# One PSUM tile of eight banks in place of two fixed pools, casts on GpSimd in halves, and a new order of work

## The chip, the cores and the metric

The kernel runs on one core of a Trainium2 chip. The time is that of one execution on the device, in microseconds (us). Five engines work side by side, each through a queue of its own in strict order: TensorE for matmuls (PE in the profile; PEld is its weight load), VectorE (DVE), ScalarE (ACT), GpSimd (POOL) and SyncE (SP), which here only issues DMAs. PE writes to PSUM, which has eight banks of 128 partitions x 512 fp32. DVE and ACT read it; POOL's operations here work on SBUF alone.

## The reference

Two steps follow each other. The first is attention over 4 batches of 8 heads, 768 positions and 64 dimensions, in which a position sees the 96 positions up to itself and the first 8 positions of its sequence, with a bias that falls with distance. The second is a feed-forward layer over all 3072 tokens, with three input matrices, of whose products the elementwise maximum is taken.

```python
scores = scale * np.matmul(q, k.transpose(0, 1, 3, 2)) - slopes * dist      # per head
scores = np.where(is_global | is_local, scores, -1e9)
a = softmax(scores)                                                          # over keys
x = np.matmul(a, v)                                  # to (3072, 512)
h = np.maximum(np.maximum(x @ w1, x @ w2), x @ w3)   # 512 -> 768
out = h @ w_out                                      # 768 -> 512
```

Inputs and output are fp32; the matmuls take bf16.

## The kernel before

Tokens are cut into 24 tiles T of 128 (six for each batch), and two neighbouring tiles make a pair G. The feed-forward layer takes the tiles in seven chunks of 4, 2, 2, 4, 4, 4 and 4 tiles, so that attention for a chunk must be done before its first feed-forward matmul.

The order is written out: SCHEDULE is a list of some 760 units that a planner has put in order, and the last lines of the function call one short function for each. A unit is a letter, its arguments and, behind "@", the buffer that it takes. On each engine the instructions run in the order of the list; semaphores between engines are put in by the tile framework. So a unit waits for its inputs, for its buffer to be released, and for everything ahead of it in its engine's queue. Where the last argument chooses the engine, 0 is ACT, 1 is DVE and 2 is POOL.

The units, by the line of their main instruction:

- l (lines 190 and 197): load of q, k or v (first argument 0 for q, 1 for k, 2 for v) for a pair, 512 KB. "12" as the pair stands for the first 512 positions of batch 0, which are loaded in four pieces (q and k, each in two halves of heads).
- c (205, 210): cast of a load to bf16. v (215): the same for half a tile of v.
- x (229, 235): eight PE transposes of a cast half into a PSUM bank. y (243, 246): copy of that to SBUF as qkT. From pair 5 on X (251) is used instead, a transposing DMA.
- S (301): scores of a tile for half of the heads (g), eight 64-row matmuls into two banks; four for the first tile of a batch. Where its last argument is 1, two matmuls with a bias come first (293), and no m follows.
- e (308): exp of the scores on ACT, into P. m (317, 319): P times a mask on DVE. K (330) and B (325) make masks and biases at the start.
- G (266, 268) and V (279, 281): the eight global rows of k and v, kept or put in the place of rows that the next tile doesn't need. So G of a tile waits for its S, and V of a tile for its A.
- A (343, 346): P times v, sixteen matmuls of 65 columns into two banks. n (354, 355): the result divided by the row sums, into xb.
- t (370) and u (373): four PE transposes of xb and a copy to xT; Z (376) is a transposing DMA that does the same.
- F (385): one sixth f of the width of one of the three products j of a chunk, four matmuls 512 wide (256 wide in the two short chunks) into one bank. f: for j = 0 a copy to SBUF (399), for j = 1 (401) and j = 2 (404) the maximum with it, always on DVE.
- O (409): output of a tile, six matmuls. o (424): its copy, s its store. E (406 to 415): the outputs of the last chunk.
- w, W (466, 470) and q, Q (475, 478): load and cast of the feed-forward weights. D, d (484): dummy matmuls on zeros, where PE would wait. R: the start of the mask's distances.

So "F0.4.0@3" is chunk 0, sixth 4, product 0, into bank 3 of its pool.

Two pools share PSUM. Pool "h" has four slots of one bank, for F, O, x, t and D; pool "sp" has two slots of two banks, for S, A and d:

```python
pools[name] = ctx.enter_context(tc.tile_pool(name=f"p_{name}", bufs=1, **space))
...
return pools[name].tile(shape, dtype, name=label, tag=f"{name}{slot}")
```

The first F of chunk 0 needs attention of tiles 0 to 3 and the first weights; until then the order holds the casts, transposes, S, A and so on of four tiles. Behind it F and O fill PE, with S, A, x and t of the coming chunks put between them.

Of the kernel before, what the change touches and what calls it, by code (L numbers as in the profile page):

```python
# [24 lines left out]
    l1.12.0@0 l0.12.0@1 R K3 K7 K4 B1.0 K2 K6 K1 K0 K5 B5.1 B3.1 B0.0 c1.12.0.1@0 B2.1 l1.12.1@2 l0.12.1@3  # L25
    c0.12.0.1@1 B7.1 l2.0.2@0 v1.0.2 v0.1.2 l2.1.2@1 v0.0.2 l1.2.2@4 D10.512@0 D1.256@1 x12.1.0@1 y0.1.0.0@0
    v1.1.2 y1.1.0.1@1 D3.256@2 x12.0.0@2 l0.2.2@5 y0.0.0.0 S0.0.1@0 c1.12.1.1 e0.0@0 S1.0.0@1 w0.0@0
    c0.12.1.1 v3.1.2 w0.1@1 x12.1.1@3 D5.256@0 x12.0.1@0 v2.1.2 e1.0@1 y0.1.1.0 w0.2@2 y0.0.1.0 d4.256@0
    S0.1.0@0 G0.0 e0.1@2 v3.0.2 S1.1.0@1 v2.0.2 c1.2.2.2@2 e1.1@3 w1.0@0 y1.1.1.1 y1.0.0.1 y1.0.1.1 w1.1@1
    l2.2.2@2 G1.1 D3.256@1 S2.0.1@0 e2.0@4 m0.1.1 D2.256@1 A0@1 m1.0.1 n0@0 D3.256@1 S2.1.0@0 m1.1.1 G2.0  # L30
    e2.1@5 D2.256@1 S3.1.0@1 t0@1 m2.1.1 e3.1@6 u0.1@0 D4.256@3 A1@0 n1@1 S3.0.1@1 c0.2.2.1 l0.3.2@6 V1.0
    D2.256@3 A2@0 V2.2 x2.1.2@3 e3.0@7 w1.2@2 m3.1.1 x2.0.2@2 y2.1.2.0@2 A3@1 n2@2 W0.1.2 V3.2 t2@0 n3@3
    u2.1 y2.0.2.0 W0.0.2 t1@1 D4.256@3 t3@3 W2.0.2 G3.0 u1.0 l1.3.2@0 u3.1 B4.0 S4.0.0@0 S4.1.0@1 e4.1@0
    G4.0 W1.1.2 v4.1.2 q2@1 m4.1.1 e4.0@2 W0.2.0 F0.0.1@2 F0.1.1@0 F0.1.0@1 F0.0.0@3 f0.1.0.1@0 l2.3.2@0
    m4.0.1 f0.0.0.0@1 S5.1.0@1 v4.0.2 S5.0.0@0 F0.0.2@1 f0.1.1.1 F0.1.2@3 F0.4.0@0 e5.0@1 f0.0.1.1
    f0.0.2.1@0 f0.1.2.1 W1.0.0 e5.1@3 m5.0.1 W2.1.1 l1.4.2@1 F0.5.0@2 f0.5.0.1@2 c0.3.2.2@0 v5.0.0 v5.1.0
# [49 lines left out]
"""  # L86

SIZES = [4, 2, 2, 4, 4, 4, 4]
RINGS = {'r': 7, 'rv': 3, 'qb': 3, 'qkT': 4, 'sp': 2, 'h': 4, 'P': 8, 'xb': 4, 'xT': 3, 'wst0': 3, 'wst1': 3, 'ht': 2, 'h01': 5, 'rz': 4}

LAST_BANKS = (1, 3, 0, 2)


@with_exitstack
def kernel(
# [43 lines left out]
    def ring(name, slot, shape, dtype, label):  # L139
        assert 0 <= slot < RINGS[name]  # L140
        return pools[name].tile(shape, dtype, name=label, tag=f"{name}{slot}")
# [422 lines left out]
```

## Time and profile before

| | |
|---|---|
| runs of the kernel before | 177.62, 178.47 and 178.69 us, median 178.47 |
| the profiled execution | 178.06 us, of which its span 176.3 |
| granted TensorE clock in it | 0.999 |
| busy: PE, DVE, ACT, POOL | 166.8, 131.2, 107.6, 46.1 us |
| first feed-forward matmul (L385) | starts at 23.52 us |
| last copy on ACT (L414) | starts at 173.04 us |
| HBM read and written | 25.17 MB and 6.29 MB, 178 GB/s over the span |

The span is one execution as the profiler saw it; the time of the execution is 1.8 us more. In the rows of the profile, times are us from the start of the span unless ns is said. A timeline row gives start, length, engine, line, operation and operands, how many instructions are merged in it, and in brackets how long the engine had been idle and what ended that. A row of busy time by stage gives the stretch and its length, then busy time and instructions of PE, PEld, DVE, ACT and POOL, then the granted clock, the DMA engines' busy share and GB/s. The chain of waits goes back from the last instruction, at each step to what released it; "issue" in it is time in which nothing that the profile shows was waited for. A matmul's length includes the time for which it still runs while the next has been started, so PE's queue is read by steps from start to start.

### The profile page before, as it was taken

To read this page: it belongs to the slowest core of one execution; us is meant where nothing else is said; L and a number is where in the kernel's file an instruction comes from. 1 tells how busy PE (TensorE), PEld (TensorE's weight loads), DVE (VectorE), ACT (ScalarE), POOL (GpSimd) and SP (SyncE) were. 2 spreads that over 40 slices of the span, in tenths; PEclk is the share of its full clock that TensorE was granted. 3 is DMA by queue.
4 is the path that set the end of the run, shared out by engine and by line. 5 is a ranking of instruction groups with operands and counts; after the bars stand their busy time and mean duration, and the time that the engine had idled before them with its cause. 6 is when DMAs were issued, how large, how long until landed. Compare 5 with 4: busy or idle time off the path is not lost.

```text
span 176.3 us, 3882 instructions
## 1 busy us (share of the span) xinstructions
PE 166.8 (95%) x1504; PEld 94.3 (53%) x1525; DVE 131.2 (74%) x258; ACT 107.6 (61%) x166; POOL 46.1 (26%) x72
## 2 busy tenths in 40 slices
PE   7689899999999999999999999999999999999992
PEld 2366644567866776744545545544445465444441
DVE  6589849888797979685899658997668996155830
ACT  5978988674999868856688587535236551211022
POOL 4039864716245462000203701130201021000000
PEclk9999999999999999999999999999999999999999
DMA  4999999999996998599999799997893136442006
GB/s 138 355 292 313 363 376 291 357 303 329 305 278 118 200 259 150 69 354 290 260 267 228 160 166 276 274 167 213 165 238 49 30 119 93 173 163 81 4 25 215
DMA packets 66627, 37.49 MB, mean 213 GB/s; under 512 B 24624, under 2 KB 61360, under 8 KB 66608
## 3 DMA queue, kind: packets, MB, share of 16 engines
q1 hardware_dynamic: 66464, 37.17, 85.0%
q8 instruction: 12, 0.20, 0.5%
q10 hardware_dynamic: 144, 0.07, 0.1%
q14 instruction: 7, 0.06, 0.1%
HBM read 25.17 MB, written 6.29 MB: 178 GB/s over the span
## 4 chain that ended last, share of the span: by engine, by line
PE 77%; DMA 8%; ACT 5%; DVE 5%; issue 2%; POOL 1%; ACTq 0%
PE h L385 45%; PE po L409 18%; PE sp L301 6%; DMA qkT<-qb 4%; DMA rawv<-in_v_dram 4%; PE op L343 2%; PE op L346 2%; ACT wmask L330 2%; ACT P L308 2%; DVE xb L355 1%; PE tp L235 1%; POOL va L279 1%; DVE ht L404 1%; PE xtp L370 1%; PE tpq L229 1%
## 5 line engine op out<-in xcount | busy, mean ns | idle before, releaser
L385 PE MATMUL h<-xT,w 128*128 128x512 bf16 (+1 forms) x491 | 98.5, 348 | 1.1 <-issue 0.2
L385 PEld LDWEIGHTS <-w 128*128 128x128 bf16 x504 | 47.3, 98 | 42.0 <-issue 1.0
L308 ACT ACTIVATE P<-sp 128x1024 bf16<-128x1024 f32 (+1 forms) x48 | 43.8, 953 | 14.4 <-PE sp L301 14.2
L409 PE MATMUL po<-wo,ht 128*128 128x512 bf16 (+2 forms) x148 | 32.9, 362 | 0.5 <-issue 0.2
L317 DVE TENSOR_TENSOR P<-P,wmask 128x1024 bf16<-128x1024 bf16 x38 | 27.9, 742 | 7.1 <-ACT P L308 7.0
L401 DVE TENSOR_TENSOR h<-h,h 128x512 bf16<-128x512 bf16 (+1 forms) x42 | 25.1, 606 | 10.6 <-PE h L385 7.5
L404 DVE TENSOR_TENSOR ht<-h,h 128x512 bf16<-128x512 bf16 (+1 forms) x42 | 26.5, 646 | 4.1 <-PE h L385 3.2
L399 ACT CAST h<-h 128x512 bf16<-128x512 f32 (+1 forms) x24 | 12.7, 538 | 22.6 <-PE h L385 22.4
L215 POOL CAST va<-rawv 64x512 bf16<-64x512 f32 x20 | 15.3, 769 | 28.0 <-DMA rawv<-in_v_dram 15.1
L409 PEld LDWEIGHTS <-ht 128*128 128x128 bf16 x156 | 14.0, 98 | 13.9
L355 DVE TENSOR_TENSOR xb<-op,rz 128x512 bf16<-128x512 f32 x24 | 16.6, 692 | 0.8
L399 DVE CAST h<-h 128x512 bf16<-128x512 f32 (+1 forms) x18 | 10.7, 597 | 8.6 <-PE h L385 8.3
L279 POOL COPY va<-vaf 4x260 int32<-4x260 int32 x20 | 9.3, 467 | 26.2 <-PE op L346 25.0
L301 PE MATMUL sp<-qkT 64*128 64x128 bf16 x352 | 14.5, 218 | 1.3 <-ACT qkT L243 0.8
L301 PEld LDWEIGHTS <-qkT 64*128 64x128 bf16 x352 | 10.0, 94 | 9.6 <-issue 6.1
L343 PEld LDWEIGHTS <-P 128*128 128x128 bf16 x192 | 12.5, 97 | 2.8 <-issue 0.6
L424 ACT COPY ost<-po 128x512 f32<-128x512 f32 x15 | 8.8, 590 | 8.3 <-PE po L409 8.3
L343 PE MATMUL op<-va,P 128*128 128x65 bf16 x160 | 12.4, 193 | 0.1
L346 PEld LDWEIGHTS <-P 128*128 128x128 bf16 x160 | 10.4, 97 | 1.5
L484 PE MATMUL wp<-zeros 128*128 128x256 bf16 (+1 forms) x43 | 9.6, 353 | 1.2 <-DVE cap L502 1.2
L346 PE MATMUL op<-va,P 128*128 128x65 bf16 x128 | 9.9, 193 | 0.5 <-POOL va L279 0.5
L414 ACT COPY ost<-po 128x512 f32<-128x512 f32 (+2 forms) x5 | 2.3, 481 | 10.6 <-PE po L409 10.4
(69 smaller groups left out, 128.6 us busy)
## 6 DMA issues: line engine op xcount, KB each, us to landing
rawv<-in_v_dram SPq DMA_DIRECT2D x12, 512.0 KB, 7.3
out_dram<-ost SPq DMA_DIRECT2D x23, 256.0 KB, 2.5
rawk<-in_k_dram SPq DMA_DIRECT2D x10, 512.0 KB, 7.3
rawq<-in_q_dram SPq DMA_DIRECT2D x10, 512.0 KB, 7.3
wst<-in_moe_w_dram SPq DMA_DIRECT2D x3, 1024.0 KB, 10.4
wst<-in_moe_w_dram SPq DMA_DIRECT2D x3, 512.0 KB, 7.8
wost<-in_moe_w_out_dram SPq DMA_DIRECT2D x3, 512.0 KB, 6.6
rawqk<-in_k_dram SPq DMA_DIRECT2D x2, 512.0 KB, 5.3
```

What stands on the lines that cost most here:

```text
L215: copies[how](heads(va(T))[64 * e:64 * e + 64, :, 0:D], src)
L301: nc.tensor.matmul(sp[:, hh, j2, ds], qT(T - ds, 1)[hsl, jp], qT(T, 0)[hsl, jp], start=not how, stop=True, skip_group_check=True)
L308: nc.scalar.activation(P[:, :, 0:n], sps[T, g].rearrange("p a b d n -> p (a b) d n")[:, :, 0:n], AF.Exp, bias=0.0, scale=scale)
L317: mul(P, P, wmask[:, g, :, 0:2])
L343: nc.tensor.matmul(o, P[:, i, 0], heads(va(T))[:, h], start=True, stop=(t == 0), skip_group_check=True)
L346: nc.tensor.matmul(o, P[:, i, 1], heads(va(T - 1))[:, h], start=False, stop=True, skip_group_check=True)
L355: nc.vector.tensor_tensor(out=x.rearrange("p (g h) d -> p g h d", g=2), in0=o4[:, :, :, 0:64], in1=rz[:, :, :, None].to_broadcast([128, 2, ...
L385: nc.tensor.matmul(ps, w123[f // 2][:, j, dm, (f % 2) * 128:(f % 2) * 128 + 128], xT[c][:, dm], start=(dm == 0), stop=(dm == 3))
L399: copies[how](h01, ps)
L401: nc.vector.tensor_max(h01s[c, f], h01s[c, f], ps)
L404: nc.vector.tensor_max(dst, h01s[c, f].rearrange("p (t e i) -> p t e i", e=2, i=64), ps.rearrange("p (t e i) -> p t e i", e=2, i=64))
L409: nc.tensor.matmul(po, ht[c][:, f, tt * 128:(tt + 1) * 128], wo[:, f, cols], start=(f == 0), stop=(f == NF - 1))
```

## The change

Four things change, and none of them changes the arithmetic or the size of an operation on PE, DVE or ACT.

1. PSUM is one tile of eight banks. A unit of pool "h" takes any one bank and a unit of pool "sp" any two neighbouring ones; the number behind "@" is now the bank.
2. c, W and Q on POOL are issued as two instructions, each over half of the first free dimension.
3. The list of units is new: the order on every queue, the engine of some units, and the banks. By kind, the changes in number are: D and d from 12 units (43 matmuls) to 9 (34), Z from 16 to 14, t and u from 8 to 10, m from 45 to 44 with one more biased S. By engine: f of j = 0 from 24 on ACT and 18 on DVE to 19 and 23; o from 15 on ACT and 5 on DVE to 12 and 8; c on POOL from 8 to 10 and on DVE from 10 to 8; v on POOL, ACT and DVE from 24, 16 and 8 to 22, 22 and 4; V from 10, 5 and 1 to 12, 2 and 2; W on POOL from 5 to 4, Q on POOL from 2 to 1.
4. The last outputs take the banks in another order.

```diff
-RINGS = {'r': 7, 'rv': 3, 'qb': 3, 'qkT': 4, 'sp': 2, 'h': 4, 'P': 8, ...
-LAST_BANKS = (1, 3, 0, 2)
+RINGS = {'r': 7, 'rv': 3, 'qb': 3, 'qkT': 4, 'sp': 2, 'h': 8, 'P': 8, ...
+LAST_BANKS = (3, 4, 7, 6, 5, 0, 1, 2)
...
-        space = {"space": bass.MemoryType.PSUM} if name in ("sp", "h") else {}
-        pools[name] = ctx.enter_context(tc.tile_pool(name=f"p_{name}", bufs=1, **space))
+        if name not in ("h", "sp"):
+            pools[name] = ctx.enter_context(tc.tile_pool(name=f"p_{name}", bufs=1))
...
+    banks = ctx.enter_context(tc.tile_pool(name="banks", bufs=1, space=bass.MemoryType.PSUM))
+    psum = banks.tile([128, 8, 512], FP32, name="psum")
+
     def ring(name, slot, shape, dtype, label):
+        if name in ("h", "sp"):
+            n = 1 if name == "h" else 2
+            assert 0 <= slot <= 8 - n
+            flat = psum[:, slot:slot + n].rearrange("p b x -> p (b x)")
+            if dtype == BF16:
+                flat = flat.bitcast(BF16)
+            flat = flat[:, 0:math.prod(shape[1:])]
...
+    def cast(how, dst, src):
+
+        n = src.shape[1]
+        for lo, hi in (((0, n // 2), (n // 2, n)) if how == 2 else ((0, n),)):
+            copies[how](dst[:, lo:hi], src[:, lo:hi])
...
-            copies[how](dst, raw[a, G, p].rearrange("i (j s) (e d) -> i j e s d", s=2, e=4))
+            cast(how, dst, raw[a, G, p].rearrange("i (j s) (e d) -> i j e s d", s=2, e=4))
...
-        copies[how](dst, raw[a, G, p].rearrange("i (j s) (e d) -> i j e s d", s=2, e=2))
+        cast(how, dst, raw[a, G, p].rearrange("i (j s) (e d) -> i j e s d", s=2, e=2))
...
-        copies[how](w123[g][:, j], src)
+        cast(how, w123[g][:, j], src)
...
-        copies[how](wo[:, 2 * i:2 * i + 2], wst["o", i])
+        cast(how, wo[:, 2 * i:2 * i + 2], wst["o", i])
```

Of the list, the beginning up to chunk 0, before:

```text
    l1.12.0@0 l0.12.0@1 R K3 K7 K4 B1.0 K2 K6 K1 K0 K5 B5.1 B3.1 B0.0 c1.12.0.1@0 B2.1 l1.12.1@2 l0.12.1@3
    c0.12.0.1@1 B7.1 l2.0.2@0 v1.0.2 v0.1.2 l2.1.2@1 v0.0.2 l1.2.2@4 D10.512@0 D1.256@1 x12.1.0@1 y0.1.0.0@0
    ...
    l2.2.2@2 G1.1 D3.256@1 S2.0.1@0 e2.0@4 m0.1.1 D2.256@1 A0@1 m1.0.1 n0@0 D3.256@1 S2.1.0@0 m1.1.1 G2.0
    e2.1@5 D2.256@1 S3.1.0@1 t0@1 m2.1.1 e3.1@6 u0.1@0 D4.256@3 A1@0 n1@1 S3.0.1@1 c0.2.2.1 l0.3.2@6 V1.0
    D2.256@3 A2@0 V2.2 x2.1.2@3 e3.0@7 w1.2@2 m3.1.1 x2.0.2@2 y2.1.2.0@2 A3@1 n2@2 W0.1.2 V3.2 t2@0 n3@3
    u2.1 y2.0.2.0 W0.0.2 t1@1 D4.256@3 t3@3 W2.0.2 G3.0 u1.0 l1.3.2@0 u3.1 B4.0 S4.0.0@0 S4.1.0@1 e4.1@0
    G4.0 W1.1.2 v4.1.2 q2@1 m4.1.1 e4.0@2 W0.2.0 F0.0.1@2 F0.1.1@0 F0.1.0@1 F0.0.0@3 f0.1.0.1@0 l2.3.2@0
```

and after:

```text
    l1.12.1@0 l0.12.1@1 l1.12.0@2 R K4 K7 B1.0 l0.12.0@3 K2 B3.1 B2.1 c1.12.1.1@0 l2.0.2@0 v1.0.2
    c0.12.1.1@1 v0.1.2 l0.2.2@4 B0.0 D10.512@0 x12.1.1@0 y0.1.1.1@0 D3.256@1 x12.0.1@1 K5 y0.0.1.1 v0.0.2 K0
    D5.256@2 S0.1.0@2 l2.1.2@1 l1.2.2@5 S1.1.0@4 y1.1.1.0@1 w0.0@0 y1.0.1.0 w0.1@1 K6 c1.12.0.1 D2.256@0
    x12.1.0@0 v1.1.2 w0.2@2 c0.12.0.1 D3.256@1 x12.0.0@1 y1.1.0.1 y0.1.0.1 w1.0@0 y1.0.0.1 l2.2.2@2
    c0.2.2.2@2 e0.1@0 e1.1@1 v2.1.2 v2.0.2 y0.0.0.0 m1.1.1 G0.0 w1.1@1 S1.0.1@2 G1.0 m0.1.1 S0.0.1@4
    S2.1.0@0 e1.0@2 S2.0.1@6 G2.1 e2.1@3 D4.256@2 A1@0 w1.2@2 c1.2.2.2 e0.0@4 A0@2 e2.0@5 S3.1.0@4 e3.1@6
    S3.0.1@6 e3.0@7 m2.1.1 V1.1 n0@0 D3.256@2 A2@2 V2.2 n1@1 t0@0 t1@1 v3.0.0 v3.1.0 m3.1.1 G3.2 l1.3.2@6
    n2@2 x2.0.2@4 y2.0.2.0@2 u0.1@0 x2.1.2@5 D2.256@2 A3@2 u1.0 y2.1.2.1 W0.0.2 n3@3 t2@0 S4.0.0@4 S4.1.0@6
    e4.0@1 G4.2 W0.1.2 D2.256@1 t3@1 K3 K1 l0.3.2@0 S5.0.0@2 e5.0@2 e4.1@0 u2.1 S5.1.0@4 e5.1@4 W2.0.0 u3.1
    F0.0.0@0 F0.1.0@1 F0.0.1@2 F0.1.1@3 V3.1 f0.1.0.1@0 W0.2.2 f0.0.0.0@1 l0.4.2@1 m5.0.1 W1.0.2 v4.1.0
    F0.1.2@1 F0.0.2@4 m4.1.1 m5.1.1 f0.1.1.1 F0.4.0@3 f0.4.0.0@2 v4.0.0 F0.2.0@0 l2.3.2@0 f0.2.0.0@3
    f0.0.1.1 W1.1.0 F0.3.0@5 v5.0.2 m4.0.1 v5.1.2 q2@0 A4@2 f0.1.2.1@0 F0.5.0@0 W2.1.1 f0.0.2.1 F0.5.1@1
```

More of the change, by code (lines that the diff above doesn't have):

```diff
@@ L86 @@
+    s5.1 F6.5.1@1 F6.5.2@2 f6.5.0.1@4 f6.5.1.1 f6.5.2.1 E@2
 """
 SIZES = [4, 2, 2, 4, 4, 4, 4]
[L89 to L91 removed]
+RINGS = {'r': 7, 'rv': 3, 'qb': 3, 'qkT': 4, 'sp': 2, 'h': 8, 'P': 8, 'xb': 4, 'xT': 3, 'wst0': 3, 'wst1': 3, 'ht': 2, 'h01': 5, 'rz': 4}
+LAST_BANKS = (3, 4, 7, 6, 5, 0, 1, 2)
 @with_exitstack
```

125 lines of the change are left out of this document (64 added, 61 removed).

## The prediction

> **What bounds the kernel now.** I read the page first (busy times, then the forty slices), then the busy time by stage, then the chain of waits around the only long pause of TensorE, then what PE waits for.
>
> ```profile
> span 176.3 us, 3882 instructions
> PE 166.8 (95%) x1504; PEld 94.3 (53%) x1525; DVE 131.2 (74%) x258; ACT 107.6 (61%) x166; POOL 46.1 (26%) x72
> ...
> PE   7689899999999999999999999999999999999992
> ...
> PEclk9999999999999999999999999999999999999999
> ```
>
> PE is busy for 95% of the span, at the full granted clock, and its gaps lie in the first slices. Busy time by stage says how much is left behind them (PE is the first number after the stretch's length):
>
> ```profile
> 10.00:23.50 13.50, 12.12 (x193) 8.56 (x191) 11.51 (x22) 11.62 (x18) 10.84 (x15) 1.00 1.13 332
> 23.50:60.00 36.50, 36.22 (x355) 23.26 (x361) 29.65 (x57) 30.27 (x44) 16.47 (x20) 1.00 1.06 285
> 60.00:100.00 40.00, 39.26 (x374) 23.09 (x378) 32.95 (x66) 27.48 (x43) 10.05 (x17) 1.00 1.06 228
> 100.00:140.00 40.00, 39.37 (x327) 19.68 (x331) 31.33 (x57) 21.93 (x33) 5.16 (x10) 1.00 0.84 178
> 140.00:173.00 33.00, 32.75 (x215) 16.23 (x216) 19.15 (x33) 8.46 (x14) 1.82 (x4) 1.00 0.33 100
> ```
>
> From 23.5 to 173 PE idles 0.28 + 0.74 + 0.63 + 0.25 = 1.9 us in 149.5. That is all that a better supply of banks can win there. So the kernel is a head of 23.5 us, a dense stretch of 149.5, and 3.3 us for the last copy and store. The head ends when chunk 0's first F starts, and the chain of waits says what that stands on:
>
> ```profile
> 17.98 0.99 POOL qb L210
> 18.97 0.60 issue
> 19.57 0.81 POOL va L279
> 20.37 0.05 issue
> 20.42 0.41 POOL va L279
> ...
> 20.87 0.19 PE op L346
> ...
> 21.77 0.70 DVE xb L355
> ...
> 22.51 0.40 PE xtp L370 x4
> 22.91 0.55 PE sp L301 x16
> ...
> 23.52 0.38 PE h L385
> ```
>
> A whole POOL cast (c1.2.2.2, 0.99) stands before POOL's V2; A3 waits for that, then n3, t3, the two S of tile 4, and F0 starts.
>
> **The change, part by part.** Durations are rows of the profiled execution. Where a queue has work waiting I use the step from one start to the next: DVE 0.61 for a 512-wide f and 0.60 for an unhindered m (28.90 shows two f in 1.39), ACT 0.92 for an exp of 1024 (15.61: two in 1.93), PE 0.216 for a 512-wide matmul.
>
> *PSUM as one tile.* Arithmetic and sizes stay. In the order of the changed kernel's instructions each wait on PSUM names the last reader of the same bank, so one tile adds no wait between banks. But the new order does not use eight banks to stay further behind the readers. Counting PE work between two uses of a bank behind the first F, 34 of 212 units come back within 1.5 us before and 59 after. A bank read by a 512-wide f on DVE is free 0.96 us after PE goes on: 0.16 for which the last matmul still runs (0.379 long, steps of 0.216), 0.68 for f, two handovers of 0.06. F5.5.0 follows F5.0.0 on bank 0 after one F, 0.86: PE waits 0.10. F1.4.2 follows S6.0 on bank 0 after 0.67, and the half exp needs 0.60 + 0.28: 0.2. With every reader prompt, such shortages are 0.4 us at 10 places before and 1.3 at 18 after: +0.9 us. Ends: -1.9 (all idle time goes) and what a late reader makes of it (below).
>
> *The readers.* f and o move from ACT to DVE (102 to 107, 5 to 8), u rises by 2; v falls by 4, c by 2. From the first F to the first F of chunk 3, my sum of steps in DVE's queue is 38.5 before and 42.7 after, against 50.4 and 49.3 of PE work. While that 6.6 us of cover lasts this costs nothing; it costs where several DVE steps stand ahead of one bank.
>
> *PE work moved.* Behind the first F: S5.0 and S5.1 go into the head (16 matmuls, 0.45 us); t7 and t10 come in for two transposing DMAs (2 x 0.22, rows "xtp x4 0.22"), 0.45. Every run of S among F costs 0.22 beyond its matmuls: 16 take 0.55 and 8 take 0.33 in the chain, so 0.11 fixed, and the six O matmuls behind a run take 1.40 instead of 1.29. Runs there fall from 19 to 16, 0.65. The two DMAs that go took 3.0 each on SP's queue, hidden. Sum: -0.45 + 0.45 - 0.65 = -0.65 us. The end (E on other banks) keeps its 3.3 us, as PE has no pause from 168 on. In the head one more S is biased (two 512-wide matmuls, 0.43) and nine 256-wide dummies go (0.109 each, 0.98); both lie in waits for ACT.
>
> *POOL's casts in halves.* Fifteen casts become thirty. Before has no 128x512 cast on POOL; bounds: half of 1.04, so nothing is added, and the 128x128 cast's 0.36 with the slope to 1.04 gives 0.65 each, 0.26 more per cast. I take 0.65 (nearest in kind): 15 x 0.26 = 3.9 us on an engine that is busy for 46 of 176. On the path it counts only in the head (c1.2.2.2 before V2.2; W0.0, W0.1). The gain is on DVE:
>
> ```profile
> 54.46 0.69 DVE L317 TENSOR_TENSOR P<-P,wmask 128x1024 bf16<-128x1024 bf16 x1 [1.27 <-ACT P L308]
> 55.07 1.11 DVE L210 CAST qb<-rawq 128x1024 bf16<-128x1024 f32 x1
> 56.10 1.09 DVE L317 TENSOR_TENSOR P<-P,wmask 128x1024 bf16<-128x1024 bf16 x1
> ```
>
> The m takes 0.69 alone and 1.09 when a POOL v is in progress (54.65 to 56.65): it waits out POOL's instruction. Halves shorten the longest such wait from about 1.0 to 0.6. But most POOL operations met in this way are v's, which stay whole, so I take 0.3 us of DVE time, off the path.
>
> The Trainium skill, SBUF — State Buffer, "Who interferes with whom", says that the second of the two engines to issue is shut out until the first has finished, so it speaks against halves too: DVE can step in between them. By that rule c1.2.2.2 would end one m (0.68) later, V2.2 at 20.2 instead of 19.5 (below), and the sum would be up to 0.3 more, 178.4; I go by the rows.
>
> *The head.* The loads keep their pace (the first four land at 5.04, 6.55, 8.1 and 9.5; then about one 512 KB per 1.5). Queue by queue in the new order: the last head cast ends at 10.2, its transposes at 10.9; three copies on DVE (0.61 each) reach 12.1; y0.0.0.0 on ACT must follow on the same bank, 12.7; G0 and S1.0 reach 13.1, where ACT starts an unbroken queue: five full exps, one half, 13.3 + 5 x 0.92 + 0.5 = 18.4; v3.0 and v3.1, now on ACT, 2 x 0.63, 19.65. POOL (c1.2.2.2 in halves from 17.2, V2.2 to 19.5) is just ahead of that. A3 ends at 20.6, n3 at 21.5, t3 at 21.95, S5.0 at 22.25; S5.1 needs the banks of e4.0 (22.2), so F0 starts at 22.65. On POOL, G4 now waits for S4.1 (21.45) with W0.1 and W0.2 queued behind it: 21.8 + 4 x 0.65 = 24.4, for F units due at 24.4 and 26.1, so W0.1 (23.1) has 1.3 to spare. Three m in this queue can each meet a POOL step: 0 to 3 x 0.4; I take 0.4. Head 23.0, -0.5.
>
> *SP's queue.* v0 stays fifth, q2 goes ahead of v1; v2 goes ahead of w1.1. At 1.5 us per 512 KB, w1.1 (8 MB) lands where v2 did, 17.0 + 12.9 = 29.9. DVE's W2.1.1 waits for it, with f0.0.2.1 and n4 queued behind; F0.5.1, 9.1 us behind the first F (32.1), needs it. 29.9 + 1.1 leaves 1.1 us.
>
> *New waits.* F0.4.0 takes bank 3 at 5.18 us behind the first F. f0.1.1.1 frees it, behind f0.1.0.1 and three m on DVE: 1.73 + 0.1 + 0.61 + 3 x 0.60 + 0.61 = 4.85, a margin of 0.3. POOL runs W halves and v's just then; each m hit adds up to 0.4. Three hits make PE 0.9 late, one or none nothing; I take 0.3, for one or two.
>
> **Sum.** 176.3 - 0.5 (head) - 0.65 (PE work) + 0.9 (banks) + 0.3 (new wait) = 176.35 of span; the profiled execution took 178.06, 1.76 more than its span, so 178.1. It stood 0.4 under the median, 178.47. I say 178.1.
>
> **The rivals.**
> 1. *The head pays in full and the shortages don't show*: 178.06 - 0.9 (head at 22.65) - 0.65 - 0.3 (of the 1.9 idle) = 176.2. For it: fewer S runs, PE idle for only 1.9 us with a fixed split of the banks. Against: banks used more tightly, DVE's fuller queue. 0.22.
> 2. *Slower: DVE becomes late in chunk 0.* All three m meet a POOL step (PE late by 0.9, not 0.3), and W2.1.1 waits for w1.1. It decides from the point where w1.1 lands after 31.0; each us beyond is a us of PE. The worst row is w1.2 before, 23.92 + 10.4 = 34.3: late by 3.3. I take 2.2; with the head's gain gone (+0.5), 178.1 + 0.6 + 2.2 + 0.5 = 181.4. For it: DMA stands at 1.06 to 1.13 of its share up to 60 us. Against: 8 MB had landed at 29.9. 0.18.
> 3. *A transposed load is late.* X12 and X22 have 4.8 us of PE work between their cast and their S (6.1 at least before); landings range from 3.8 to 7.8. One late by 1.5: 179.6. 0.12.
> 4. *The clock drops.* PE going round eight banks in short bursts could lose its clock. Before granted 1.00 in every stage, against this. A lapse like the start, where ten 512-wide dummies took 0.43 instead of 0.216 each, costs 2.2; two give 182.5. 0.02. The Trainium skill, TensorE: Matmul & The Clock Gate, "A second HAM failure mode: psum-queue depth-cycling", describes such a loss; no row here shows it.
> 5. *The change doesn't do what it says*: the tile is one for the waits, and PE waits for a reader at every unit; 48 S by 0.6 alone give 207. The waits in the built program speak against it. 0.01.
>
> **How the numbers follow.** My case has 0.45, by itself 177.0 to 179.3 (head 22.65 to 23.5, new waits 0 to 0.9, shortages 0.4 to 1.9). A measurement of this kernel tells about 1% from no change, so 176.7 and 180.25 are the borders. Faster: most of rival 1 (0.19) and 0.02 of mine, 0.21. Slower: most of rival 2 (0.16), 0.03 of rival 3, rivals 4 and 5: 0.22. Same: 0.57. The range leaves out about a tenth at either end: 176.0 to 180.9.
>
> **What would show it.** Right: F0 starts between 22.6 and 23.4; from there to the last matmul 149 to 151 us; granted clock 1.00; POOL casts of 128x512 near 0.65; DVE busier, ACT less. Short PE waits on DVE for its bank show the shortages, one near 28 us the new wait; DVE idle before W's cast shows rival 2; PE's S waiting for a qkT transpose near S12 or S22 shows rival 3. I am wrong if F0 starts after 24, or if PE idles more than 4 us behind it.

## The result, and the profile after

The changed kernel takes 180.57 us, median of 4 runs (180.13 to 180.81), against 178.05 (177.59 to 178.69) for the kernel before in the same comparison: 1.0137 times as long, 95% interval 1.0092 to 1.0181. The forecast was 178.1 and no change that a measurement can tell; the time lies inside the range that it gave (176.0 to 180.9), near the upper end, but the change made the kernel 1.4% slower. The profiled execution's span grew from 176.3 to 178.9. Its first feed-forward matmul (now line 406) starts at 23.64, where it started at 23.52, and its last matmul at 175.40 instead of 172.74. So the head is as long as before, the last store too, and the dense stretch in between grew from 149.2 to 151.75 us.

The page of the changed kernel, in the lines that answer to those of before:

```profile
span 178.9 us, 3899 instructions
PE 169.0 (94%) x1526; PEld 94.6 (53%) x1526; DVE 135.5 (76%) x268; ACT 101.7 (57%) x152; POOL 48.0 (27%) x92
...
PE   7868898999989999999999998999999999999992
...
PEclk9999999999999999999999999999999999999999
```

Nothing here looks like a loss of 2.5 us: the clock is full, DVE gained 4.3 us of work and ACT lost 5.9, as forecast. Busy time by stage (PE, PEld, DVE, ACT, POOL behind the length) is no louder:

```profile
10.00:23.50 13.50, 10.85 (x193) 7.83 (x191) 11.70 (x23) 11.03 (x16) 10.28 (x18) 1.00 1.13 329
23.50:60.00 36.50, 35.23 (x330) 21.77 (x325) 31.05 (x61) 26.47 (x37) 16.05 (x28) 1.00 1.01 283
60.00:100.00 40.00, 39.84 (x403) 23.90 (x402) 33.80 (x69) 27.37 (x42) 8.46 (x18) 1.00 1.03 210
100.00:140.00 40.00, 39.47 (x314) 19.42 (x313) 31.68 (x58) 20.40 (x31) 8.96 (x16) 1.00 0.81 182
140.00:173.00 33.00, 32.96 (x220) 15.94 (x219) 20.18 (x35) 7.72 (x13) 2.47 (x6) 1.00 0.30 97
```

PE's idle time behind the first F is 1.27 + 0.16 + 0.53 + 0.04 = 2.0 us, and it was 1.9. That is a trap: a 512-wide matmul is 0.38 us long at steps of 0.216, so it holds some 0.16 us for which it still runs while the next one has been started, and a pause of up to 0.16 before a matmul is booked as busy. A count of the steps from one matmul's start to the next shows what the busy time hides: beyond its matmuls' own pace (0.216 us for one 512 wide), and outside the runs of S, PE stood 3.9 us behind the first F. In the first two runs further down, which keep the old order, it is 1.2 and 1.1. (The trace of the kernel before misses some matmul records, so they stand in for it.) Three of the pauses are long. What PE waited for names them:

```profile
PE psum L505 <- DVE xb L376: 1.1, 1, 1.1
PE psum L406 <- DVE h L422: 0.7, 1, 0.7
...
PE psum L406 <- DVE ost L445: 0.5, 1, 0.5
PE psum L256 <- DVE ht L425: 0.5, 1, 0.5
```

The first line lies in the head. The others are, by steps, 0.85 us (F0.4.0 at 29.68), 0.65 (F4.4.2 at 111.76) and 0.64 (x4.1.2 at 50.20). Each time PE wants a bank whose reader (f0.1.1, o3.3, f1.4.2) stands on DVE behind other steps. F0.4.0 is the place that the forecast named (all engines, from 26 us on):

```profile
25.57 0.69 DVE L420 CAST h<-psum 128x512 bf16<-128x512 f32 x1 [1.11 <-PE psum L406]
...
25.80 3.19 PE L406 MATMUL psum<-xT,w 128*128 128x512 bf16 x14
26.30 2.73 DVE L338 TENSOR_TENSOR P<-P,wmask 128x1024 bf16<-128x1024 bf16 x3
26.83 1.65 POOL L236 CAST va<-rawv 64x512 bf16<-64x512 f32 x2 [0.62 <-DMA rawv<-in_v_dram]
...
28.95 1.27 DVE L422 TENSOR_TENSOR h<-h,psum 128x512 bf16<-128x512 bf16 x2
29.68 0.59 PE L406 MATMUL psum<-xT,w 128*128 128x512 bf16 x2 [0.69 <-DVE h L422]
```

Three masks m take 2.73 us instead of 1.8, as POOL casts beside them. f0.1.1 can start only at 28.95, and PE gets bank 3 at 29.68.

In the head, the chain of waits shows why nothing was won:

```profile
15.07 0.66 DVE P L338
15.73 0.34 issue
16.07 0.70 DVE va L302
...
16.80 0.68 DVE va L302
...
17.75 0.70 DVE xb L376
18.45 0.04 issue
18.49 0.49 PE psum L505 x3
```

The two copies of V1 (line 302) moved four rows of 520 numbers each, and took 0.70 each. DVE's division for A1 and A0 waited for them, and PE's dummies for the division.

### The profile page after: what moved, and what is told of

Read it like the earlier page. It is cut to its first block, busy times and chain, and to the rows that moved or that the text cites. A ratio compares the mean times of both kernels' runs of the same rounds, so it can differ in the third digit from the quotient of the medians.

```text
span 178.9 us, 3899 instructions
## 1 busy us (share of the span) xinstructions
PE 169.0 (94%) x1526; PEld 94.6 (53%) x1526; DVE 135.5 (76%) x268; ACT 101.7 (57%) x152; POOL 48.0 (27%) x92
## 4 chain that ended last, share of the span: by engine, by line
PE 74%; DVE 11%; ACT 5%; issue 2%; ACTq 0%; DVEq 0%
PE psum L406 45%; PE psum L430 16%; PE psum L322 5%; ACT P L329 4%; DVE P L338 3%; PE psum L364 3%; PE psum L367 2%; DVE ht L425 2%; PE psum L256 2%; DVE h L422 1%; PE psum L391 1%; DVE va L236 1%; DVE va L302 1%; DVE P L340 1%; PE psum L505 1%
## 5 line engine op out<-in xcount | busy, mean ns | idle before, releaser
L406 PE MATMUL psum<-xT,w 128*128 128x512 bf16 (+1 forms) x504 | 100.1, 348 | 1.3 <-DVE h L422 0.7
L329 ACT ACTIVATE P<-psum 128x1024 bf16<-128x1024 f32 (+1 forms) x48 | 43.4, 952 | 10.9 <-PE psum L322 9.8
L422 DVE TENSOR_TENSOR h<-h,psum 128x512 bf16<-128x512 bf16 (+1 forms) x42 | 24.9, 604 | 13.7 <-ACT h L420 9.0
L430 PE MATMUL psum<-wo,ht 128*128 128x512 bf16 (+2 forms) x156 | 33.7, 363 | 0.0
L425 DVE TENSOR_TENSOR ht<-h,psum 128x512 bf16<-128x512 bf16 (+1 forms) x42 | 26.4, 644 | 0.9 <-PE psum L406 0.5
L420 DVE CAST h<-psum 128x512 bf16<-128x512 f32 (+1 forms) x23 | 13.4, 592 | 5.9 <-PE psum L406 5.9
L376 DVE TENSOR_TENSOR xb<-psum,rz 128x512 bf16<-128x512 f32 x24 | 16.6, 691 | 0.8
L322 PE MATMUL psum<-qkT 64*128 64x128 bf16 x352 | 14.5, 217 | 1.8 <-ACT qkT L264 1.4
L236 ACT CAST va<-rawv 64x512 bf16<-64x512 f32 x20 | 12.3, 618 | 0.3
L364 PE MATMUL psum<-va,P 128*128 128x65 bf16 x160 | 12.4, 193 | 0.0
```

Source lines behind the costliest of these rows:

```text
L236: copies[how](heads(va(T))[64 * e:64 * e + 64, :, 0:D], src)
L322: nc.tensor.matmul(sp[:, hh, j2, ds], qT(T - ds, 1)[hsl, jp], qT(T, 0)[hsl, jp], start=not how, stop=True, skip_group_check=True)
L329: nc.scalar.activation(P[:, :, 0:n], sps[T, g].rearrange("p a b d n -> p (a b) d n")[:, :, 0:n], AF.Exp, bias=0.0, scale=scale)
L364: nc.tensor.matmul(o, P[:, i, 0], heads(va(T))[:, h], start=True, stop=(t == 0), skip_group_check=True)
L376: nc.vector.tensor_tensor(out=x.rearrange("p (g h) d -> p g h d", g=2), in0=o4[:, :, :, 0:64], in1=rz[:, :, :, None].to_broadcast([128, 2, ...
L406: nc.tensor.matmul(ps, w123[f // 2][:, j, dm, (f % 2) * 128:(f % 2) * 128 + 128], xT[c][:, dm], start=(dm == 0), stop=(dm == 3))
```

## The experiments

Seventeen kernels ran. Ratios are to the kernel before, timed beside each, with 95% intervals. In the variants on the one tile the line numbers are up to one lower than those of the changed kernel; the two kernels of DVE rows at the end have lines of their own.

**The tile alone.** The list of before on the one tile, with casts whole.

```diff
-    ... A0@1 m1.0.1 n0@0 D3.256@1 S2.1.0@0 m1.1.1 G2.0 ...
+    ... A0@6 m1.0.1 n0@0 D3.256@1 S2.1.0@4 m1.1.1 G2.0 ...
-        for lo, hi in (((0, n // 2), (n // 2, n)) if how == 2 else ((0, n),)):
+        for lo, hi in (((0, n // 2), (n // 2, n)) if False else ((0, n),)):
```

> The list of the kernel before, on the one PSUM tile: slots of the h pool on banks 0 to 3, those of the sp pool on 4 to 7, casts whole. Theory N (the loss comes from the new list: more DVE steps ahead of each bank, banks taken back sooner, DVE held up by POOL): 178.1, no change beyond 0.5. Rival T (one tile makes PE wait across banks): 180 or more, with waits of PE for readers of other banks. If the tile alone gave a gain, it would be below 177.5.

Measured: 178.43 us, 1.0009 (0.9983 to 1.0035). The tile adds no wait that shows; the interval leaves room for 0.35%.

**The halves alone.** The kernel before, its pools and its list, with c, W and Q on POOL in two instructions.

```diff
-        copies[how](w123[g][:, j], src)
+        cast(how, w123[g][:, j], src)
```

> The list and the pools of the kernel before, with POOL's casts of c, W and Q in halves. Theory N: within 0.6 of before (177.6 to 178.6), POOL's head cast c1.2.2.2 about 0.25 longer, the first F at 23.5 to 23.8. Rival H (the halves cost: thirty POOL instructions meet DVE more often and POOL's V2 comes later): 179 or more, first F after 24.

Measured: 178.23 us, 1.0007 (0.9982 to 1.0032). On the old order, halves change nothing that shows.

**The changed kernel with whole casts.**

```diff
-        for lo, hi in (((0, n // 2), (n // 2, n)) if how == 2 else ((0, n),)):
+        for lo, hi in (((0, n // 2), (n // 2, n)) if False else ((0, n),)):
```

> The changed kernel with POOL's casts whole again, nothing else. Theory N: about as slow as the changed kernel, 180.0 to 181.0; the m in the queue ahead of f0.1.1.1 still take 0.8 to 1.0 each, as two POOL v's and a W cast run beside them. Rival H: 179 or less. If the halves help as meant: 181 or more.

Measured: 183.86 us, 1.0313 (1.0271 to 1.0355). Theory N and rival H both miss; what is left is the third case, that the halves help as meant, and by far more than the 181 that it began with. On the new order whole casts cost 1.8%, 3.1 us (3.3 by the medians): F0 starts at 24.43, and the pause of 0.64 near 50 us becomes 2.77. The timeline (DVE and POOL) shows one mask behind it:

```profile
48.65 2.85 DVE L340 TENSOR_TENSOR P<-P,wmask 128x512 bf16<-128x512 bf16 x1
...
48.65 0.61 POOL L236 CAST vaf<-rawv 64x512 bf16<-64x512 f32 x1
49.21 1.03 POOL L183 CAST wo<-wost 128x1024 bf16<-128x1024 f32 x1
50.19 1.03 POOL L183 CAST qb<-rawq 128x1024 bf16<-128x1024 f32 x1
```

It started with POOL's first cast and came through only when all three were done. In the changed kernel the same mask took 0.43:

```profile
47.86 0.43 DVE L340 TENSOR_TENSOR P<-P,wmask 128x512 bf16<-128x512 bf16 x1
```

**Three DVE steps put ahead of masks**, in the three places of the long pauses.

```diff
-    F0.1.2@1 F0.0.2@4 m4.1.1 m5.1.1 f0.1.1.1 F0.4.0@3
+    F0.1.2@1 F0.0.2@4 m4.1.1 f0.1.1.1 m5.1.1 F0.4.0@3
...
-    ... v7.0.1 e7.1@6 F1.4.2@0 F1.3.2@1 m6.1.1 e7.0@7 F1.3.1@6 f1.4.2.1 F1.0.0@7
+    ... e7.1@6 F1.4.2@0 F1.3.2@1 e7.0@7 F1.3.1@6 f1.4.2.1 v7.0.1 m6.1.1 F1.0.0@7
...
-    ... m17.1.1 m18.0.1 v18.1.2 m19.0.1 f4.2.0.0@2 A16@0 v19.0.0 v19.1.0 V16.2 o3.3.1@1
+    ... m17.1.1 o3.3.1@1 m18.0.1 v18.1.2 m19.0.1 f4.2.0.0@2 A16@0 v19.0.0 v19.1.0 V16.2
```

> The changed kernel with three places of DVE's queue changed and nothing else: f0.1.1.1 ahead of m5.1.1; f1.4.2.1 ahead of v7.0.1 and m6.1.1; o3.3.1 ahead of m18.0.1 and what follows. Theory N: the three PE pauses of 0.63, 0.64 and 0.65 near 29.7, 50.2 and 111.8 us shrink to 0.1 or less each, 1.5 to 1.9 in all: 178.7 to 179.1. Rival (a PE pause taken out in one place comes back in the next, since DVE is full): less than 0.7 gained, 179.9 or more.

Measured: 180.26 us, 1.0112 (1.0068 to 1.0156). The first pause is gone, but in place of the other two A6 and A18 now stand (0.8 and 0.4 us in what PE waited for, 0.93 and 0.54 by steps). The lines name DVE's copy into qkT and its division into xb. A reads neither: by the list, A6 takes the bank that y4.1.2 has still to read, and A18 the banks that n16 has still to read. An order that only shuffles DVE's steps moves the wait from one bank to the next.

**Work taken off DVE** in the same places.

```diff
-    ... f0.1.0.1@0 W0.2.2 f0.0.0.0@1 l0.4.2@1 m5.0.1 W1.0.2 ... m5.1.1 f0.1.1.1
+    ... m5.0.1 f0.1.0.1@0 W0.2.2 f0.0.0.0@1 l0.4.2@1 W1.0.2 ... f0.1.1.1 m5.1.1
...
-    ... y3.1.2.0@3 ... v7.1.1 ... v7.0.1 ...
+    ... v7.1.0 v7.0.0 y3.1.2.0@3 ...
...
-    ... v17.1.1 ... m18.0.1 ... o3.3.1@1
+    ... v17.1.2 ... o3.3.1@1 m18.0.1 ...
```

> The changed kernel with DVE's work thinned out ahead of the three long pauses, not only put in another order: m5.0 moves into DVE's idle 1.11 us ahead of f0.1.0, f0.1.1 ahead of m5.1; v7.1 and v7.0 go from DVE to ACT's idle 1.78 us at 43.9; v17.1 goes from DVE to POOL, and o3.3 ahead of m18.0. Theory D (DVE is full in these three places, so work has to leave it): the three pauses of 0.85, 0.64 and 0.65 go and do not come back near by, the dense stretch falls from 151.75 to 150.0 or less, 178.6 to 179.2 us. Rival R (the list is tight everywhere and pauses wander, as they did when only the order was changed): 180.0 or more, with new pauses within a few us behind the old places.

Measured: 179.83 us, 1.0095 (1.0072 to 1.0119), dense stretch 150.70. Between the two theories: 1.05 us of the dense stretch came back. Of the second pause 0.28 stayed. In place of the third, A18 stands 0.46 us for the banks that n16 reads; n16 comes late, as o3.3, moved ahead of masks that stand before n16, keeps DVE idle for 0.85 us until a store has released its buffer.

**V1 on POOL.**

```diff
-    ... c1.2.2.2 e0.0@4 ... m2.1.1 V1.1 n0@0
+    ... V1.2 c1.2.2.2 e0.0@4 ... m2.1.1 n0@0
```

> The changed kernel with V1 on POOL ahead of its cast c1.2.2.2 instead of on DVE, where its two copies took 1.41 us while POOL ran. Theory H (the forecast gain of the head is lost where DVE waits out POOL): the division n0 starts at 16.2 to 16.5 instead of 17.5, F0 at 23.1 to 23.3 instead of 23.64, the time falls by 0.3 to 0.5 to about 180.1. Rival: V2 on POOL, now later by 1.0, takes over as what A3 waits for, and F0 stays at 23.5 or later: 180.5 or more.

Measured: 180.48 us, 1.0130 (1.0102 to 1.0158). The theory holds for the head: F0 starts at 23.14, half a us earlier, as the division (line 374, then 375) starts at 16.11 instead of 17.50:

```profile
15.06 1.13 DVE L337 TENSOR_TENSOR P<-P,wmask 128x1024 bf16<-128x1024 bf16 x1
16.11 0.20 DVE L374 RECIPROCAL rz<-psum 128x8 f32<-128x8 f32 x1
16.34 0.69 DVE L375 TENSOR_TENSOR xb<-psum,rz 128x512 bf16<-128x512 f32 x1
```

The dense stretch then gave 0.4 of it back, in the pause near 50 us (1.14 instead of 0.64), so that the time fell by 0.1 and not by the 0.3 to 0.5 that was expected.

**Other banks, chosen wrongly.** Order and engines of the changed kernel, and then of the kernel before on the tile, with each unit on the bank that had been free longest, if every reader follows its matmuls at once.

```diff
-    ... F4.5.0@1 e17.0@6 v16.1.0 F4.4.0@4 ... F4.3.2@5
+    ... F4.5.0@3 e17.0@6 v16.1.0 F4.4.0@6 ... F4.3.2@4
```

> The changed kernel, order and engines as they are, but each unit takes the bank (or the two neighbouring ones) that has been free longest, instead of the bank of the list. By my count of PE's work between two uses of a bank, the shortages behind the first F fall from 1.3 to 0.6 us with every reader prompt, and from 18.5 to 5.6 us if every reader were 0.6 late. Theory B (a late DVE costs time only because banks come back too soon): the short pauses and the ones of 0.85 and 0.65 go, that at 50 us shrinks, the dense stretch falls by 1.5 to 2.5, 178.1 to 179.1. Theory D (DVE's queue is late also for qkT, xb and the others that have nothing to do with banks): less than 0.6 is won, 180.0 or more.

> The order and the engines of the kernel before on the one tile, whole casts, with each unit on the bank that has been free longest: by the same count 0.01 us of shortage with prompt readers (0.37 with the banks of the kernel before) and 1.05 with readers 0.6 late (9.6). Theory: the idle time of PE behind the first F in the kernel before is 1.1 to 1.8, of which at most a third waits for banks, so 0.2 to 0.6 is won: 177.3 to 177.8. Rival: free banks let PE run ahead until it stands at data instead, nothing is won, 178.0 to 178.4.

(In the second kernel the casts are in halves, not whole as its expectation says.)

Measured: 193.92 us, 1.0895 (1.0866 to 1.0924), and 192.49 us, 1.0817 (1.0780 to 1.0855). Both are some 14 us slower than the kernel whose order they keep, which neither expectation had in view. The longest pause of the first shows how (PE, then ACT):

```profile
115.25 1.02 PE L405 MATMUL psum<-xT,w 128*128 128x512 bf16 x4 [1.63 <-ACT ost L444]
```

```profile
114.61 0.59 ACT L444 COPY ost<-psum 128x512 f32<-128x512 f32 x1
```

These four matmuls are F4.3.2. It was sent to the bank of O3.1, whose copy o3.1 stands twenty units behind O3.1 in the list; on ACT two exp, a v and an f came first. In the changed kernel F4.3.2 takes the bank of S17.1, which was free by then. My count held the bank of O3.1 for free after 0.6 us. It is free when its reader's turn comes.

**Banks by the readers' ends.** The same order and engines once more; now a bank counts as free from the end of its last reader in the kernel's own trace, and the units were given banks so that few start soon after that. Only the numbers behind "@" of PE's units differ from the changed kernel, and LAST_BANKS.

```diff
-    F0.1.2@1 F0.0.2@4 ... F0.4.0@3
+    F0.1.2@4 F0.0.2@3 ... F0.4.0@6
...
-LAST_BANKS = (3, 4, 7, 6, 5, 0, 1, 2)
+LAST_BANKS = (4, 1, 6, 5, 7, 0, 3, 2)
```

> The changed kernel, order and engines as they are, with other banks, chosen by when the last reader of each bank ended in the changed kernel's trace (the recoloured list of before took a reader to follow its matmuls at once; o and f units that stand late in the list then held banks that PE was sent to). In the trace PE starts 47 units within 0.12 us of their bank's release; with these banks 19 would. Theory B (a late DVE costs time mostly because banks come back too soon): the dense stretch falls from 151.75 to 149.5 to 150.3, 178.3 to 179.1 us. Theory D (queues, not banks): under 0.6 is won, 180.0 or more.

Measured: 178.03 us, 1.0004 (0.9988 to 1.0021), a little better than the theory of the banks asked for. F0 starts at 23.46, the dense stretch is 149.07 us. Of what PE waited for, all waits of line 405 for a bank behind DVE's h, ht and ost are gone; what is left of any size is

```profile
PE psum L321 <- ACT qkT L263: 1.4, 1, 1.4
PE psum L504 <- DVE cap L522: 1.2, 1, 1.2
PE psum L363 <- ACT P L328: 0.6, 1, 0.6
PE psum L249 <- DVE qbq L182: 0.6, 1, 0.6
PE psum L321 <- DVE xb L375: 0.4, 1, 0.4
```

most of it in the head. So other bank numbers, with nothing else changed, take the whole loss away.

**All three, and the old order on wide banks.** First the relief of DVE, V1 on POOL and banks by the readers; a second version with the banks chosen again from its own trace; and the order and engines of the kernel before on the tile, casts in halves, with banks by the readers' ends in that order's trace.

```diff
-    ... D10.512@0 D1.256@1 x12.1.0@1 ...
+    ... D10.512@5 D1.256@0 x12.1.0@6 ...
-LAST_BANKS = (1, 3, 0, 2)
+LAST_BANKS = (0, 2, 5, 4, 6, 7, 1, 3)
```

> The changed kernel with DVE relieved in three places (as in the run that gave 1.05 us of the dense stretch), V1 on POOL (which gave 0.5 us of the head) and banks by the readers' ends. If the three add: F0 at 23.1, dense stretch 149 to 149.6, 177.2 to 178.0 us, so level with the kernel before or a little faster. Rival: the head's gain is given back at 50 us, where POOL's casts then meet the masks, and the banks add nothing: 179.0 to 179.8.

> The version with DVE relieved, V1 on POOL and wide banks (177.67 us), with banks chosen anew from its own trace, in which the pause of 0.88 us before A16 stood on a bank that o3.1 held. If that pause goes: 176.8 to 177.2. Rival: it comes back behind DVE, 177.5 to 177.9.

> The order and engines of the kernel before on the one tile, casts in halves, banks chosen by the readers' ends in its own trace: 3 units would start within 0.12 us of their bank's release, 22 did with its own banks. Theory: the kernel before has some 0.5 us of idle time that banks cause, so 177.3 to 177.8 us. Rival: 178.0 to 178.4, as PE then stands at data; what the tile is worth to this order is nothing.

Measured: 177.67 us, 0.9984 (0.9972 to 0.9996); 178.07 us, 0.9998 (0.9974 to 1.0022); and 177.10 us, 0.9967 (0.9938 to 0.9997). The first came out where its expectation had the three adding (F0 at 23.00, dense stretch 149.53, 177.67 us). Against other banks alone, though, the head gained 0.46 and the dense stretch lost 0.46, and the ratio is 0.2% better. A pause of 0.88 us is new in it. It stands before A18, not A16: A18 has the banks that n16 reads, and n16 is late because DVE, with o3.3 moved ahead, stands idle until a store has released o3.3's buffer:

```profile
108.46 0.69 DVE L444 COPY ost<-psum 128x512 f32<-128x512 f32 x1 [1.65 <-DMA out_dram<-ost]
```

The second version gave A18 the banks of A16 again, so the pause stayed (0.96); it did not try what its expectation says. The third is the fastest by the median, and a little faster than its theory, though only 0.3% faster than the kernel before, with the interval's upper end close to 1. In its busy time by stage PE is without a pause that shows from 23.5 to 60 and from 100 to 140 us:

```profile
23.50:60.00 36.50, 36.50 (x365) 23.52 (x363) 30.25 (x59) 30.50 (x45) 18.25 (x30) 1.00 1.08 289
60.00:100.00 40.00, 39.75 (x391) 23.10 (x388) 32.37 (x64) 27.26 (x43) 10.44 (x19) 1.00 1.06 226
100.00:140.00 40.00, 40.00 (x326) 19.54 (x322) 31.70 (x58) 22.05 (x33) 5.13 (x11) 1.00 0.85 176
```

**Whole casts on the wide banks**, to see whether what POOL does to DVE costs time only through banks.

```diff
-        for lo, hi in (((0, n // 2), (n // 2, n)) if how == 2 else ((0, n),)):
+        for lo, hi in (((0, n // 2), (n // 2, n)) if False else ((0, n),)):
```

> The changed kernel's order with the banks chosen by the readers' ends (178.03 us) and POOL's casts whole again. With the changed kernel's own banks, whole casts cost 3.3 us. Theory B (what POOL does to DVE reaches PE only through banks that come back too soon): here they cost under 1.0, 178.0 to 179.0. Theory D (the masks' lateness itself holds up A and the transposes): 2 us or more, 180.0 or more.

Measured: 180.54 us, 1.0139 (1.0111 to 1.0167). The theory that it passes only through banks falls: whole casts cost 1.35%, 2.4 us, here too (1.0139 against 1.0004). F0 starts at 24.47, a us later, since V1's two copies take 2.36 instead of 1.41, and the same mask near 48 us takes 2.84, so that A6 stands 1.2 us behind DVE (DVE, then PE):

```profile
47.84 2.84 DVE L339 TENSOR_TENSOR P<-P,wmask 128x512 bf16<-128x512 bf16 x1
50.72 0.43 DVE L235 CAST va<-rawv 64x512 bf16<-64x512 f32 x1
51.17 0.86 DVE L339 TENSOR_TENSOR P<-P,wmask 128x512 bf16<-128x512 bf16 x1
51.95 0.43 DVE L424 TENSOR_TENSOR ht<-h,psum 128x256 bf16<-128x256 bf16 x1
```

```profile
52.44 0.43 PE L363 MATMUL psum<-vaf,P 128*128 128x65 bf16 x8 [1.20 <-DVE ht L424]
```

The line named is f1.4.2, which reads A6's bank. But A6 needs the second mask too, and that ended at 52.03. So of the pause, 1.37 by steps, about 1.0 would stand on any bank; and in the head the transposes wait for the xb that they read.

**Three places alone.** Nine bank numbers of the changed kernel, around the three long pauses.

```diff
-    F0.1.2@1 F0.0.2@4 ... F0.4.0@3 ... F0.2.0@0
+    F0.1.2@6 F0.0.2@7 ... F0.4.0@0 ... F0.2.0@4
-    ... x4.1.2@0 F1.5.1@2 ... F4.4.1@4 ... F4.4.2@2 ... F4.0.1@4
+    ... x4.1.2@2 F1.5.1@5 ... F4.4.1@7 ... F4.4.2@4 ... F4.0.1@2
```

> The changed kernel with nine bank numbers changed, so that F0.4.0, x4.1.2 and F4.4.2, before which PE stood 0.85, 0.64 and 0.65 us, take banks that had been free for 1.3, 0.9 and 2.1 us. If the three pauses are what the banks cost: 178.6 to 179.2. If the many short ones behind them are as much, or the pauses come back at the next tight bank: 179.5 to 180.2. My middle value is 179.3, since x4.1.2 is followed by A6, which waits for a qkT that DVE delivers late whatever the bank.

Measured: 179.36 us, 1.0088 (1.0057 to 1.0119), on the middle value. The three pauses are gone, and no wait of A6 for DVE's qkT is left, so that wait, which the expectation held for independent of the bank, was one for a bank as well. Something like half of the loss went with the pauses: by the ratios 0.9 of 2.4 us, by the dense stretches of the profiled executions (150.26, against 151.75 and the 149.07 of wide banks) 1.5 of 2.7. The rest must be the many short ones; no run took them alone.

**The old order on tight banks**, the reverse test: the order and engines of the kernel before on the tile, each unit on a bank that was released shortly before.

```diff
-    ... S2.0.1@4 e2.0@4 m0.1.1 D2.256@1 A0@6 ...
+    ... S2.0.1@3 e2.0@4 m0.1.1 D2.256@0 A0@1 ...
-LAST_BANKS = (1, 3, 0, 2)
+LAST_BANKS = (3, 5, 1, 2, 4, 6, 7, 0)
```

> The order and engines of the kernel before on the one tile, casts in halves, with banks taken again almost as soon as they are free: by the trace of that order on its own banks PE would start 41 units within 0.12 us of their bank's release and 144 within 1 us (22 and 131 with its own banks; 47 and 154 in the changed kernel), and planned waits stay under 0.2 us in all. Theory B: tight banks alone cost 1.5 to 2.5 here too, 179.6 to 180.6. Theory D (they cost where DVE is full, which it is less here): under 1.0, 178.0 to 179.0.

Measured: 179.66 us, 1.0090 (1.0062 to 1.0117), against 0.9967 with wide banks: 1.2% on the old order as well, where DVE has more room. Not all of it is certainly banks: one of its pauses, 0.8 us, is an S that waits for a transposing DMA. The run of the tile alone has a wait of that kind, 0.8 us, too and stands at 1.0009, so a difference of 0.8% to that run is left without it.

**DVE beside POOL by itself.** Two kernels that leave out everything of the reference and run only rows of DVE steps, alone and beside rows of POOL casts, one execution each.

```diff
+        phase(m, 6, None, 0)
+        phase(m, 8, whole, 7)
+        phase(m, 8, half, 7)
...
+        phase(vcopy, 6, None, 0)
+        phase(vcopy, 10, whole, 7)
+        phase(vcopy, 10, half, 7)
```

> Only the disputed cost, nothing of the reference is computed: a row of masks on DVE (tensor_tensor, 128x1024 bf16, SBUF alone) by itself, then beside back-to-back POOL casts of 128x1024, of the same in halves, and of 64x512; then a row of maxima with a PSUM operand (as f) by itself, beside whole casts and beside halves. Theory H (DVE's SBUF-only steps wait for a gap in POOL's work, and find one only now and then while POOL has work queued): beside whole casts some masks take 2 us or more, beside halves most take under 1.3; those of f stay at 0.6 to 0.7 in all three. Rival (they take turns, one POOL instruction for one of DVE): every mask beside whole casts takes about 0.68 + 1.0, beside halves 0.68 + 0.6, and none more.

> Only disputed costs, nothing of the reference is computed: the strided mask of a batch's first tile (128x512 of a 128x1024 tile) by itself, beside whole POOL casts, beside halves; the pair of v's cast and that mask on DVE beside POOL's mix of a 64x512 cast and two whole casts, and beside the same with the whole ones in halves; V's copy of 4x520 by itself, beside whole casts and beside halves. Theory T (turns, one for one, whatever the form): mask and copy take their own time plus the rest of one POOL instruction, so at most 0.43 + 1.0 and 0.28 + 1.0 beside whole casts, 0.43 + 0.6 and 0.28 + 0.6 beside halves. Theory L (a short or strided DVE step can lose the turn several times): some take 2 us or more beside whole casts.

Measured, in the first kernel's timeline of DVE: six masks alone, eight beside seven whole casts, eight beside halves, then the maxima of f alone and beside whole casts:

```profile
5.93 4.32 DVE L42 TENSOR_TENSOR P<-P,wmask 128x1024 bf16<-128x1024 bf16 x6
...
10.28 10.91 DVE L42 TENSOR_TENSOR P<-P,wmask 128x1024 bf16<-128x1024 bf16 x8
...
21.35 7.91 DVE L42 TENSOR_TENSOR P<-P,wmask 128x1024 bf16<-128x1024 bf16 x8
...
43.24 4.28 DVE L45 TENSOR_TENSOR h<-h,ps 128x512 bf16<-128x512 bf16 x6
...
47.56 5.74 DVE L45 TENSOR_TENSOR h<-h,ps 128x512 bf16<-128x512 bf16 x8
```

A mask goes from 0.72 us (4.32 by six) to 1.36; f, whose second operand lies in PSUM, from 0.71 to 0.72. Single masks beside whole casts take 1.41, beside halves 0.98: strict turns, one POOL instruction for one of DVE. In the second kernel V's copy of 4x520, alone, beside whole casts and beside halves:

```profile
58.20 1.86 DVE L79 COPY va<-va 4x520 bf16<-4x520 bf16 x6
...
60.10 8.68 DVE L79 COPY va<-va 4x520 bf16<-4x520 bf16 x10
...
68.81 5.96 DVE L79 COPY va<-va 4x520 bf16<-4x520 bf16 x10
```

Single copies take 0.28, 1.06 and 0.58. The mask of 128x512 takes 0.43, 1.14 and 0.71. Turns hold here too: nothing took longer than its own time and that of one POOL instruction (1.53 at most, a mask beside whole casts). So theory L and the starving of theory H fall for these rows, and the 2.85 us above is not explained by them.

## Why the prediction was wrong

**Sum.** The span was to go from 176.3 to 176.35 and went to 178.9: the dense stretch came out 2.0 us above its terms and the head 0.6. The terms that failed are those of the banks, shortages and new wait, +1.2 together and 2.4 measured, and the head, -0.5 forecast and +0.12 measured. Behind the first stand two steps, that every reader is prompt and that DVE's fuller queue "costs nothing"; behind the second stands a DVE copy that meets POOL and was not counted. By the prediction's own steps:

*One tile adds no wait between banks, halves alone gain next to nothing.* Both right, on the old order: 1.0009 and 1.0007. The 128x512 cast was taken at 0.65 and took 0.67.

*Shortages, +0.9.* Failed by size. The step counted PE's work between two uses of a bank "with every reader prompt". Readers here are often not prompt: o stands in the list when ACT or DVE has room, f behind masks. The banks alone were 1.0137 against 1.0004, so 1.3% or 2.4 us. The two runs with wrongly chosen banks failed by this same step, and showed its force: 14 us by bank numbers alone. Something like half of that is in the three long pauses, of which the new wait below is one; the rest, 1.2 to 1.5, is above the 0.9 that the step had for prompt readers.

*New wait, +0.3, ends 0 and 0.9.* The place was right, and so was the mechanism: three masks that all meet POOL. It was the upper end, 0.85. But it had two like it at 50 and 112 us that the step had not looked for.

*The readers, "costs nothing" while DVE's queue has 6.6 us of cover.* This is the step that hid the other two pauses. It was a sum over 50 us. From 27 to 30 us DVE is busy for 3.00 of 3.00 us (2.90 in the kernel before), from 42 to 52 for 9.23 of 10 (8.09), from 110 to 113 for 2.96 of 3 (2.77). Cover that lies elsewhere is no cover. That DVE is full there is shown by the two runs that moved its steps: in another order the pauses moved on, with work taken away 1.05 us came back. That it needs the tight banks to cost what it did is shown by the run on wide banks, and the old order, nearly as full in two of the three places, shows no such pause.

*Head, -0.5.* Measured +0.12. The queues came as worked out up to ACT's last v (19.65 forecast, 19.70 in the trace). What failed is the allowance for POOL's collisions, "Three m in this queue can each meet a POOL step: 0 to 3 x 0.4; I take 0.4." V1 was not in it: two copies of 0.28 took 1.41, and m2.1 took 1.12, so the first division started at 17.5. With V1 off DVE F0 came at 23.14, close to the 23.0 of the forecast.

*PE work, -0.65.* Borne out in part: beyond their matmuls, the 16 runs of S cost 4.3 us in the changed kernel, the 19 of the old order 4.9 and 4.6 in the runs of the tile alone and the halves alone, 0.3 to 0.6 less. But with wide banks the new order's dense stretch is 149.07, only 0.15 below the kernel before; where the rest went was not taken apart.

*Halves, 0.3 us off the path.* Wrong on the new order, where they are worth 2.4 to 3.1 us: it puts V1 and masks beside POOL's casts where something waits for them. The row of turns explains the head's part, a us: a copy takes 0.28 by itself, and the POOL instruction that it waits for is what sets its cost. The Trainium skill, SBUF — State Buffer, "Who interferes with whom", says that a mask like this and a POOL cast shut each other out for whole instructions, and that a DVE step with at most one SBUF input, outside the two-port modes, does not contend with POOL; the rows agree (a mask 1.41 against 0.69, f unchanged at 0.69). V's copy, with one SBUF input, does meet POOL here (1.06 against 0.28). The forecast's sentence on that page had the wrong sign, up to 0.3 us against the halves: what a half costs POOL is less than what it saves DVE.

**Rivals.** The first, faster rival failed in both halves: the head did not pay and the shortages did show. The second rival, the slower one, came true in its first half (all three masks met POOL) and not in the second: no W waited for w1.1, DMA and clock were as before. No S waited for a transposed load. The tile did what it says. Of the signs that the forecast named, F0 (23.64) lies just outside 22.6 to 23.4 and the dense stretch (151.75) outside 149 to 151, while PE's idle time by steps, 3.9, stays just under the 4 that was to prove it wrong.

**Taken apart.** With halves and wide banks the new order stands at 1.0004 and the old one at 0.9967. So the new order by itself is not better than the old (first F at 23.46 against 23.15, dense stretch 149.07 against 148.52). That DVE's fuller stretches eat what its fewer runs of S and dummies save is my reading, not shown. Its banks then cost 1.3% more, and the halves save it from another 1.4 to 1.8%.

**What stays open.** Why one mask was shut out for three POOL instructions, in both runs of the new order with whole casts and nowhere else (nor in the run of the tile alone, which has whole casts on the old order). And how much of the old order's loss on tight banks is its late DMA.

## What to carry to other kernels

When fixed buffers become one pool, the choice of the buffer is a plan of its own: take one whose last reader ended well before by the trace, not by the list's order or by an ideal latency; here that choice alone was worth 2.4 us one way and cost 14 the other. When a wait names a DVE step, look in the list whether the step delivers data or only frees the bank. Read the bound engine by steps from start to start, since its busy time hid half of the loss, and check every other engine's load over the few us around each wait, not over a stage. A short DVE step on SBUF costs about what the POOL instruction beside it costs (a copy of 0.28 took 1.06 beside casts of 1.03, and 0.58 beside casts of 0.60), so keep such steps off DVE, or POOL's instructions short, where something waits.

## What the runs showed of the hardware

- In rows by themselves, DVE steps with all operands in SBUF and POOL's casts take turns, one for one: a mask of 0.69 us takes 1.41 beside casts of 1.03 and 0.98 beside casts of 0.60, and POOL's own casts grow to 1.38 and 1.07. Steps with a PSUM operand (0.69) and POOL beside them (1.04) don't notice each other.
- The cost of such a turn hardly depends on the size of the DVE step: a copy of 4x520, 0.28 alone, takes 1.06 beside whole casts, 0.78 more, and the mask of 128x1024 takes 0.72 more.
- Not expected, and not reproduced by itself: a mask of 0.43 us that waited through three POOL casts, 2.85 us, and 2.84 in a second kernel.
